# Raising the scheduling priority of the first batch's attention over weights and MoE work in a fused attention and gated-MLP kernel

## The chip, the cores and the metric

The kernel runs on one core of a Trainium2 chip. The metric is device time in microseconds (us) of one execution. Before the change three runs gave 489.43 us as the median, from 487.89 to 490.92 us. Five engines work side by side on the core, each with its own queue of instructions that it takes strictly in the order in which they were written: TensorE (PE, matmuls; PEld is its weight load), VectorE (DVE), ScalarE (ACT), GpSimd (POOL), and SyncE (SP), which here only starts transfers.

## The reference

The inputs are four batches of eight heads, 768 tokens of 64 numbers. Each query sees the 4 first tokens (sinks) and the last 128. The attention output, 768 x 512 per batch, goes through a gated MLP ("MoE" in the code).

```python
scores = scale * np.matmul(q, k.transpose(0, 1, 3, 2))
keep = is_sink | in_window                    # is_sink: pos < 4; in_window: 0 <= rel < 128
scores = np.where(keep, scores, -1000000000.0)
a = np.exp(scores - np.max(scores, axis=-1, keepdims=True))
a = a / (np.sum(a, axis=-1, keepdims=True) + 1e-09)
x = np.matmul(a, v)                           # then (B, S, H * D)
h = np.maximum(x @ w_in, 0.0)                 # 512 -> 1024
conv_out = ...                                # three taps along the tokens, weights conv_w
gate = 1.0 / (1.0 + np.exp(-conv_out))
return (h * gate @ w_out).astype(np.float32)  # 1024 -> 512
```

## The kernel before

**Attention.** The heads go in pairs, four pairs to a batch, and a pair's 768 queries in six tiles of 128, three to a half. A tile passes through three functions. `scores` multiplies on PE (tile `sc`, line 339 in the first batch, 342 and 343 later), masks and takes the minimum on DVE (lines 508 and 509), takes exponentials on ACT (512), sums and inverts on DVE (514, 515) and normalizes on POOL (517), into `pe`. `transp` turns `pe` on PE (532, tile `pts`), copies it out on ACT (534, tile `pT`) and cuts the band out of the copy with two selects on POOL (536, 538). After the third tile of a half `pv` multiplies by the values (573 and 576, tile `px`), and `xout` splits the result into a high and a low part, `xH` on ACT (350) and `xL` on DVE (351), the input of the MLP. A tile's `transp` is written one step after its `scores`, its `pv` two steps after. In batch 0 the first halves of all four pairs come first, then the second halves: 24 steps.

**Weights.** `w_in` and `w_out` come from HBM as 64-bit floats in 16 pieces of 128 x 512 (and the taps). A piece is narrowed (`narrow`: 111 on ACT; 112, 113, 114 on DVE) and split into a high part (121 on ACT) and a low part (122, `wiL` on POOL, `woL` on DVE). The list `WHEN` asks for one piece a step from step 2 on. The temporaries (`stm`) have three buffers.

**MLP.** It is cut into units of 256 tokens and 128 hidden columns: 12 matmuls into `ph` (183), the gate on ACT (190, 194, 197), DVE (195, 196, 198) and POOL (200, 201, tile `g`), and six matmuls into `po` (210) two units later. A unit of the first 256 tokens needs the first halves of all four pairs. The pieces of the units are written between the attention steps at an even rate, from the middle of batch 0 on.

**What sets the order.** The program is written in the order of the loop in `banded`, each step in three slots. A scheduler then walks through it, with a model of its own of how long things take, and fixes each engine's order: of the instructions that are ready in its model, the one with the better priority goes first, and priority is the place in the written program. What stands in a queue is never passed on the chip by what stands behind it.

Of the kernel before, what the change touches and what calls it, by code (L numbers as in the profile page):

```python
# [31 lines left out]
TRAIL = 2  # L32
NGB = TRAIL + 2
LA = 1
WHEN = list(range(2, 19))


# [360 lines left out]
def banded(c):  # L398
# [159 lines left out]
    def pv(g, t):  # L558

        s = st[g]  # L560
        hp = g % NPAIR
        hf, u = divmod(t, 3)
        if u < 2:
            return
        px = ps.tile([P, 3, P], F32, tag="px", name=f"px{g}_{hf}").rearrange("p t k -> p (t k)")
        first = 3 * hf
        tiles = range(first + 2, max(0, first - 1) - 1, -1)
        for kt in tiles:
            pT = s.pT.pop((kt, hf)).rearrange("p h a k -> p h (a k)")
            lo, hi = max(kt, first), min(kt + 1, first + 2)  # L570
            cols = slice(P * (lo - kt), P * (hi - kt) + P)
            for j in range(2):
                nc.tensor.matmul(px[D * j:D * j + D, P * (lo - first):P * (hi - first) + P], s.v[:, kt, j, :], pT[:, j, cols],  # L573
                                 start=(kt == tiles[0]), stop=False, skip_group_check=True)
        for w in range(1 - hf, 3):
            nc.tensor.matmul(px[:, P * w:P * w + P], (vsr if g >= NPAIR else c.vs)[:, w, P * hp:P * hp + P], s.sT, start=False, stop=(w == 2),  # L576
                             skip_group_check=True)
        A.xout(g, hf, px)
# [40 lines left out]
    steps = [(n, g, 3 * half + u) for n, (g, half) in enumerate(jobs) for u in range(3)]  # L619
    NST = len(steps)  # L620
    NSTB = NPAIR * T
    D1, D2 = 1, 2
# [7 lines left out]
    for i in range(NST + D2):  # L630
        if i < NST:
            n, g, t = steps[i]
            if t % 3 == 0:
                for n1, lo, hi in coming(n):
                    new = prep(n1)
                    todo += [(i + lo + (hi - lo) * (k + 1) / len(new), x) for k, x in enumerate(new)]
            if g >= NPAIR or t % 3 == 2:
                fetch()
            if t == 0 and g and g % NPAIR == 0:
                after = i + 3 if g > NPAIR else i  # L640
            if i == after:
                sink_split(c, m, vsr, g // NPAIR)
            if n + 1 < len(jobs) and (t % 3 == 2 if n < 2 * NPAIR else t == 3):
                values(n + 1)
        if i == NSTB // 2:
            clear()
        m.need(min(sum(i >= w for w in WHEN), len(m.todo)))
        for slot in range(SLOTS):
            if slot == 0 and i < NST:
                scores(g, t)  # L650
            if slot == 1 and 0 <= i - D1 < NST:
                transp(*steps[i - D1][1:])
            if slot == 2 and 0 <= i - D2 < NST:
                pv(*steps[i - D2][1:])
                if i - D2 + 1 in cuts:
                    while fill:
                        fill.pop(0)()
                    lo, hi, span = cuts[i - D2 + 1]
                    fill = m.pieces(lo, hi)
                    rate = len(fill) / (span - 0.5)  # L660
                    acc = 0.0
            acc += rate / SLOTS
            while acc >= 1.0 and fill:
                fill.pop(0)()
                acc -= 1.0
            while todo and i + (slot + 1) / SLOTS >= todo[0][0]:
                todo.pop(0)[1]()
# [143 lines left out]
```

## Time and profile before

| | us |
|---|---|
| median of three runs | 489.43 |
| the profiled execution | 490.03 |
| its span in the profile | 488.3 |
| TensorE busy in the span | 457.4 (94%) |
| VectorE busy | 348.4 (71%) |
| ScalarE busy | 340.5 (70%) |
| GpSimd busy | 312.7 (64%) |
| mean granted TensorE clock, share of full speed | 0.983 |

The span leaves 1.73 us of the profiled execution outside it. The profiled execution took 0.60 us more than the median. Busy shares are means over the whole span; the first quarter and the rest differ, so they are read by stretch.

### The profile page before, as it was taken

What the parts mean: (1) busy time and instruction counts of PE and PEld (TensorE: products, weight loads), DVE (VectorE), ACT (ScalarE), POOL (GpSimd) and SP (SyncE); (2) the same over time, 40 slices, a digit from 0 to 9 for tenths busy, and PEclk for the clock granted to TensorE, in tenths of its full rate; (3) what the DMA queues carried; (4) which work ended last, traced back from release to release, by engine and by line L of the source; (5) the groups of instructions that cost most, each with busy time, mean ns of one, the idle gap of its engine ahead of it and who ended that gap; (6) DMA issues with size and microseconds to landing.
All of it is one profiled execution on the core that took longest, in us unless ns stands there. A gap on an engine that the chain in (4) does not pass through costs nothing.

```text
span 488.3 us, 10470 instructions
## 1 busy us (share of the span) xinstructions
PE 457.4 (94%) x3149; PEld 389.7 (80%) x3149; DVE 348.4 (71%) x1212; ACT 340.5 (70%) x1086; POOL 312.7 (64%) x614
## 2 busy tenths in 40 slices
PE   2887798899999999999999999999999999999995
PEld 2555477688889888888888888888888888999993
DVE  4798989957968777786677585886675665656553
ACT  3887858778878977786877786876776754545451
POOL 3584796867976867684758577685764564344441
PEclk9988989999999999999999999999999999999998
DMA  5778653537234132334132332324021100101011
GB/s 147 211 229 212 172 168 79 126 85 188 67 72 116 61 83 66 87 96 99 60 77 58 85 81 60 70 63 98 24 55 33 44 3 0 44 2 44 1 44 53
DMA packets 87307, 41.03 MB, mean 84 GB/s; under 512 B 80160, under 2 KB 80184, under 8 KB 87240
## 3 DMA queue, kind: packets, MB, share of 16 engines
q1 hardware_dynamic: 87096, 39.99, 31.5%
q8 instruction: 28, 0.46, 0.4%
q14 instruction: 39, 0.32, 0.2%
q10 hardware_dynamic: 144, 0.26, 0.2%
HBM read 27.60 MB, written 6.29 MB: 69 GB/s over the span
## 4 chain that ended last, share of the span: by engine, by line
PE 80%; DVE 7%; DMA 3%; issue 3%; ACT 2%; POOL 2%; SPq 1%; DVEq 0%; ACTq 0%; POOLq 0%
PE po L210 27%; PE ph L183 26%; PE px L573 8%; PE sc L342 4%; PE pts L532 4%; PE sc L343 3%; PE px L576 2%; PE tq L276 2%; PE tk L294 2%; PE sc L339 2%; POOL pe L517 1%; DVE sc L508 1%; DMA wi_1r<-in_moe_w_in_dram 1%; DVE pe L509 1%; DVE stm L113 1%
## 5 line engine op out<-in xcount | busy, mean ns | idle before, releaser
L210 PE MATMUL po<-woH,g 128*128 128x512 f32 x384 | 142.0, 409 | 1.2 <-POOL g L200 1.0
L183 PE MATMUL ph<-xH,wiH 128*128 128x258 f32 (+1 forms) x384 | 112.2, 292 | 1.2 <-ACT X L255 1.2
L183 PE MATMUL ph<-xH,wiL 128*128 128x258 f32 (+1 forms) x384 | 109.0, 284 | 0.0
L183 PE MATMUL ph<-xL,wiH 128*128 128x258 f32 (+1 forms) x384 | 108.8, 284 | 0.0
L517 POOL TENSOR_SCALAR pe<-pe,sm 128x132 f32<-128x132 f32 (+1 forms) x192 | 82.8, 442 | 34.9 <-DVE sm L515 27.2
L512 ACT ACTIVATE pe<-pe,sm 128x132 f32<-128x132 f32 (+1 forms) x192 | 77.5, 406 | 15.8 <-DVE sm L509 14.7
L200 POOL TENSOR_SCALAR g<-t 128x256 fp32r<-128x256 f32 x96 | 42.2, 439 | 70.7 <-DVE t L198 50.8
L195 DVE SCALAR_TENSOR_TENSOR t<-hb,cw,t 128x256 f32<-128x256 f32 x96 | 54.0, 562 | 36.6 <-ACT t L194 36.1
L201 POOL TENSOR_TENSOR g<-t,g 128x256 fp32r<-128x256 f32 x96 | 75.2, 784 | 5.6
L210 PEld LDWEIGHTS po<-woH,g 128*128 128x128 f32 x384 | 68.7, 189 | 11.6 <-POOL g L200 2.6
L183 PEld LDWEIGHTS ph<-xH,wiH 128*128 128x128 f32 x384 | 73.0, 190 | 5.5 <-ACT X L255 1.6
L210 PE MATMUL po<-woL,g 128*128 128x512 f32 x192 | 76.4, 398 | 0.0
L183 PEld LDWEIGHTS ph<-xH,wiL 128*128 128x128 f32 x384 | 72.9, 190 | 2.1
L183 PEld LDWEIGHTS ph<-xL,wiH 128*128 128x128 f32 x384 | 72.8, 190 | 0.7
L197 ACT ACTIVATE t<-t 128x256 f32<-128x256 f32 x96 | 40.1, 418 | 33.8 <-DVE t L196 33.4
L198 DVE SCALAR_TENSOR_TENSOR t<-t,hb 128x256 f32<-128x256 f32 x96 | 47.5, 494 | 20.1 <-ACT t L197 19.0
L508 DVE COPY_PREDICATED sc<-before,sc 128x128 f32<-128x128 int32 x160 | 45.6, 291 | 22.6 <-PE sc L343 19.1
L509 DVE CUSTOM_DVE_ANT_0 pe<-sc,m 128x132 f32<-128x132 f32 (+1 forms) x192 | 54.0, 288 | 10.3 <-PE sc L343 7.8
L190 ACT ACTIVATE hb<-ph 128x258 f32<-128x258 f32 (+1 forms) x96 | 37.0, 386 | 31.4 <-PE ph L183 30.7
L536 POOL TENSOR_SCALAR_AFFINE_SELECT pT<-pT 128x256 f32<-128x256 f32 x80 | 38.2, 477 | 31.4 <-ACT pT L534 31.1
L196 DVE SCALAR_TENSOR_TENSOR t<-hb,cw,t 128x256 f32<-128x256 f32 x96 | 54.1, 564 | 4.1
L194 ACT ACTIVATE t<-hb,cw 128x256 f32<-128x256 f32 x96 | 49.2, 513 | 7.7 <-POOL g L201 3.9
(124 smaller groups left out, 930.2 us busy)
## 6 DMA issues: line engine op xcount, KB each, us to landing
raw<-in_q_dram SPq DMA_DIRECT2D x64, 96.0 KB
raw<-in_k_dram SPq DMA_DIRECT2D x64, 96.0 KB
out_dram<-stm SPq DMA_DIRECT2D x23, 256.0 KB
kk<-kk SPq DMA_DIRECT2D x24, 198.0 KB
vraw<-in_v_dram SPq DMA_DIRECT2D x24, 192.0 KB
wi_0r<-in_moe_w_in_dram SPq DMA_DIRECT2D x2, 512.0 KB
wi_1r<-in_moe_w_in_dram SPq DMA_DIRECT2D x2, 512.0 KB
wi_2r<-in_moe_w_in_dram SPq DMA_DIRECT2D x2, 512.0 KB
```

Source lines behind the costliest of these rows:

```text
L183: nc.tensor.matmul(u.h[:, 0:W], w[:, cc, ff * P:(ff + 1) * P], x[:, cc, t0:t1], start=(i == 0), stop=(i == len(prods) - 1))
L194: nc.scalar.mul(a, prev, cw[:, 0, ff:ff + 1])
L195: nc.vector.scalar_tensor_tensor(out=e, in0=this, scalar=cw[:, 1, ff:ff + 1], in1=a, op0=ALU.mult, op1=ALU.add)
L196: nc.vector.scalar_tensor_tensor(out=a, in0=nxt, scalar=cw[:, 2, ff:ff + 1], in1=e, op0=ALU.mult, op1=ALU.add)
L198: nc.vector.scalar_tensor_tensor(out=a, in0=e, scalar=1.0, in1=this, op0=ALU.add, op1=ALU.mult)
L200: nc.gpsimd.tensor_scalar(u.g[:, 0], a, 1.0, 1.0, ALU.mult, ALU.mult)
L201: nc.gpsimd.tensor_tensor(out=u.g[:, 1], in0=a, in1=f(u.g[:, 0]), op=ALU.subtract)
L210: nc.tensor.matmul(po[:, 0:c.DM], u.g[:, a, tt * P:(tt + 1) * P], w[:, ff, :], start=(ff == 0 and i == 0), stop=(ff == NFF - 1 and i == 2))
L508: nc.vector.copy_predicated(pc[:, KW:SW], before.bitcast(I32), pc[:, 0:P])
L509: nc.vector.tensor_tensor_reduce(out=pe[:, j, cols], in0=pc[:, P:SW][:, cols], in1=mk, op0=ALU.add, op1=ALU.min, scale=1.0, scalar=3.0e38, ...
L512: nc.scalar.activation(pe[:, j, cols], pe[:, j, cols], AF.Exp, bias=sm[:, j:j + 1], scale=-1.0, accum_out=sm[:, 2 + 2 * j:3 + 2 * j])
L517: nc.gpsimd.tensor_scalar(pe[:, j, cols], pe[:, j, cols], sm[:, 8 + j:9 + j], 1.0, ALU.mult, ALU.mult)
```

## The change

The body of `scores`, `transp` and `pv` is now issued inside a block that gives its instructions a priority 300 places better than where they are written, for the 24 steps of batch 0 (`NSTB` is 24). From batch 1 on the offset is 0. Nothing is added or removed: the same instructions run, with the same operands, and `transp` and `pv` still belong to tiles one and two steps back. The weights, the loading and turning of later pairs (`prep`) and the MLP's pieces keep their old priority.

```diff
+AHEAD = 300
 ...
         for slot in range(SLOTS):
-            if slot == 0 and i < NST:
-                scores(g, t)
-            if slot == 1 and 0 <= i - D1 < NST:
-                transp(*steps[i - D1][1:])
+            with c.tc.high_priority(offset=AHEAD if i < NSTB else 0):
+                if slot == 0 and i < NST:
+                    scores(g, t)
+                if slot == 1 and 0 <= i - D1 < NST:
+                    transp(*steps[i - D1][1:])
+                if slot == 2 and 0 <= i - D2 < NST:
+                    pv(*steps[i - D2][1:])
             if slot == 2 and 0 <= i - D2 < NST:
-                pv(*steps[i - D2][1:])
```

The lines of the changed kernel have numbers one higher than before (517 is 518 there). Three places follow; each shows one engine's queue, first before, then changed.

GpSimd, at the end of the first half of pair 2 (its scores are `pe_0_421`, its turned tiles 480, 531 and 561) and in the midst of pair 3's (`pe_0_545`, turned tiles 604, 654, 687). Before:

```order
L517 TENSOR_SCALAR pe_0_421<-pe_0_421,sm_166 128x132 x2
L517 TENSOR_SCALAR pe_0_545<-pe_0_545,sm_167 128x128 x2
L536 AFFINE_SELECT pT_0_0_480<-pT_1_0_531 128x2x128
L538 AFFINE_SELECT pT_1_0_531<-pT_1_0_531 128x2x128
L517 TENSOR_SCALAR pe_0_545<-pe_0_545,sm_163 128x132 x2
L536 AFFINE_SELECT pT_1_0_531<-pT_2_0_561 128x2x128
L517 TENSOR_SCALAR pe_0_545<-pe_0_545,sm_164 128x132
L538 AFFINE_SELECT pT_2_0_561<-pT_2_0_561 128x2x128
L517 TENSOR_SCALAR pe_0_545<-pe_0_545,sm_164 128x132
```

Changed:

```order
L518 TENSOR_SCALAR pe_0_421<-pe_0_421,sm_166 128x132 x2
L539 AFFINE_SELECT pT_2_0_437<-pT_2_0_437 128x2x128
L537 AFFINE_SELECT pT_0_0_480<-pT_1_0_531 128x2x128
L539 AFFINE_SELECT pT_1_0_531<-pT_1_0_531 128x2x128
L537 AFFINE_SELECT pT_1_0_531<-pT_2_0_561 128x2x128
L518 TENSOR_SCALAR pe_0_545<-pe_0_545,sm_167 128x128 x2
L539 AFFINE_SELECT pT_2_0_561<-pT_2_0_561 128x2x128
L518 TENSOR_SCALAR pe_0_545<-pe_0_545,sm_163 128x132 x2
L537 AFFINE_SELECT pT_0_0_604<-pT_1_0_654 128x2x128
L539 AFFINE_SELECT pT_1_0_654<-pT_1_0_654 128x2x128
L518 TENSOR_SCALAR pe_0_545<-pe_0_545,sm_164 128x132 x2
```

The select that finishes pair 2's last turned tile (line 538 on 561) now stands ahead of two tiles of pair 3's normalization (`sm_163`, `sm_164`), of which three instructions stood ahead of it.

GpSimd again, where the first two units of the MLP (`g_808`, `g_869`) meet the low parts of `w_in`'s second half (`stm_704` and `stm_762` are its last two pieces). Before:

```order
L122 TENSOR_TENSOR wiL<-stm_660,wiH 128x512
L517 TENSOR_SCALAR pe_1_670<-pe_1_670,sm_167 128x132 x2
L200 TENSOR_SCALAR g_808<-t_801 128x256
L201 TENSOR_TENSOR g_808<-t_801,g_808 128x256
L517 TENSOR_SCALAR pe_1_826<-pe_1_826,sm_163 128x132 x2
L200 TENSOR_SCALAR g_869<-t_862 128x256
L536 AFFINE_SELECT pT_4_1_792<-pT_5_1_847 128x2x128
L201 TENSOR_TENSOR g_869<-t_862,g_869 128x256
L122 TENSOR_TENSOR wiL<-stm_704,wiH 128x512
L538 AFFINE_SELECT pT_5_1_847<-pT_5_1_847 128x2x128
L517 TENSOR_SCALAR pe_1_826<-pe_1_826,sm_164 128x132 x2
L122 TENSOR_TENSOR wiL<-stm_762,wiH 128x512
```

Changed:

```order
L123 TENSOR_TENSOR wiL<-stm_704,wiH 128x512
L537 AFFINE_SELECT pT_4_1_792<-pT_5_1_847 128x2x128
L539 AFFINE_SELECT pT_5_1_847<-pT_5_1_847 128x2x128
L201 TENSOR_SCALAR g_808<-t_801 128x256
L518 TENSOR_SCALAR pe_1_826<-pe_1_826,sm_163 128x132 x2
L202 TENSOR_TENSOR g_808<-t_801,g_808 128x256
L123 TENSOR_TENSOR wiL<-stm_762,wiH 128x512
L201 TENSOR_SCALAR g_869<-t_862 128x256
L202 TENSOR_TENSOR g_869<-t_862,g_869 128x256
L518 TENSOR_SCALAR pe_1_826<-pe_1_826,sm_164 128x132 x2
```

The two low parts of the weights and the attention's selects now stand ahead of the MLP's `g` that they stood behind.

VectorE at the start, the first tile of pair 0 (`pe_0_206`) and the first piece of weights (`stm_257`). Before:

```order
L436 TENSOR_SCALAR m_139<-m_139 128x132
L509 ISA pe_0_206,sm_163<-sc_0_0_208,m_137 128x128
L509 ISA sm_163 128x1
L112 TENSOR_SCALAR stm_257<-stm_258 128x512
L509 ISA pe_0_206,sm_163<-sc_0_1_209,m_137 128x128
L509 ISA sm_163 128x1
L113 SCALAR_TENSOR_TENSOR stm_257<-wi_0r,stm_257 128x512
```

Changed:

```order
L437 TENSOR_SCALAR m_139<-m_139 128x132
L113 TENSOR_SCALAR stm_257<-stm_258 128x512
L510 ISA pe_0_206,sm_163<-sc_0_0_208,m_137 128x128
L510 ISA sm_163 128x1
L114 SCALAR_TENSOR_TENSOR stm_257<-wi_0r,stm_257 128x512
L510 ISA pe_0_206,sm_163<-sc_0_1_209,m_137 128x128
L510 ISA sm_163 128x1
```

Here the weights' steps moved ahead of the attention's: the first tile now stands behind the narrowing of the first piece.

Four more moves are told in words. On ScalarE the second piece's high part (line 121) now stands behind the copies of pair 2's turned queries and keys. On SyncE the load of pair 3's second half of keys now stands behind one load of values and two pieces of weights (the last of `w_in`, the fifth of `w_out`). On TensorE twelve matmuls of line 210 (units 0 and 1 of the MLP) stood ahead of the products with the values of pair 0's second half, and now stand behind them. And at the last product of batch 0's attention (`px_1_1493`) 397 instructions stand ahead of it in TensorE's queue before and after; at its low part (line 351) 332 stand ahead on VectorE before and 329 after. The last 330 rows of TensorE's queue are the same.

## Rows read from the trace of the kernel before

**Rows 1.** The page, parts 1 and 2: busy time, and tenths in 40 slices.

```profile
PE 457.4 (94%) x3149; PEld 389.7 (80%) x3149; DVE 348.4 (71%) x1212; ACT 340.5 (70%) x1086; POOL 312.7 (64%) x614
...
PE   2887798899999999999999999999999999999995
...
PEclk9988989999999999999999999999999999999998
```

**Rows 2.** By stretch: length, busy PE PEld DVE ACT POOL, granted clock, DMA.

```profile
12.20:24.40 12.20, 10.11 (x48) 7.18 (x48) 9.42 (x47) 10.90 (x39) 6.80 (x15) 1.00 0.78 211
24.40:97.60 73.20, 60.37 (x356) 45.31 (x355) 66.56 (x215) 56.19 (x178) 55.83 (x88) 0.91 0.61 164
109.40:480.00 370.60, 369.04 (x2635) 322.66 (x2635) 259.14 (x897) 259.90 (x832) 237.07 (x469) 1.00 0.24 62
```

**Rows 3.** Timeline of TensorE: start, length, line; in brackets the idle before.

```profile
41.87 2.40 PE L573 MATMUL px<-pT,vraw 128*64 128x128 f32 x12 [1.73 <-POOL pT L538]
...
50.16 1.30 PE L573 MATMUL px<-pT,vraw 128*64 128x128 f32 x12 [0.64 <-POOL pT L538]
...
57.90 0.68 PE L339 MATMUL sc<-kk,X 128*128 128x260 f32 x2 [1.67 <-DVE sm L509]
59.71 1.21 PE L339 MATMUL sc<-kk,X 128*128 128x260 f32 x2 [1.13 <-DVE sm L515]
61.63 1.21 PE L339 MATMUL sc<-kk,X 128*128 128x260 f32 x2 [0.71 <-DVE sm L509]
...
83.49 0.49 PE L318 MATMUL trk<-ident,raw 128*128 128x128 f32 x3
```

**Rows 4.** Timeline of GpSimd, around the release of pair 2's product.

```profile
38.48 1.31 POOL L517 TENSOR_SCALAR pe<-pe,sm 128x132 f32<-128x132 f32 x2 [0.86 <-ACT xH L350]
...
40.19 1.27 POOL L517 TENSOR_SCALAR pe<-pe,sm 128x132 f32<-128x132 f32 x1
41.42 0.40 POOL L538 TENSOR_SCALAR_AFFINE_SELECT pT<-pT 128x256 f32<-128x256 f32 x1
```

**Rows 5.** Busy time by stretches of 2 us, columns as in the second group.

```profile
40.00:42.00 2.00, 0.27 (x4) 0.13 (x4) 1.64 (x5) 1.57 (x4) 1.97 (x4) 0.94 1.22 287
42.00:44.00 2.00, 2.00 (x12) 1.07 (x12) 1.65 (x4) 0.79 (x2) 0.34 (x1) 0.50 0.86 258
44.00:46.00 2.00, 2.00 (x11) 1.74 (x10) 0.57 (x2) 0.59 (x2) 0.00 (x0) 0.70 1.09 265
...
62.00:64.00 2.00, 2.00 (x7) 1.51 (x7) 2.00 (x5) 0.64 (x4) 1.92 (x3) 0.50 0.36 57
64.00:66.00 2.00, 2.00 (x10) 1.67 (x9) 2.00 (x10) 1.67 (x6) 2.00 (x4) 0.58 0.55 205
```

**Rows 6.** Waits in 24 to 97 us: us in total, times, longest.

```profile
DVE stm L112 <- POOL wiL L122: 1.8, 1, 1.8
```

**Rows 7.** Timeline of GpSimd, the two low parts of the weights.

```profile
67.28 1.28 POOL L122 TENSOR_TENSOR wiL<-stm,wiH 128x512 fp32r<-128x512 f32 x1
...
70.20 1.53 POOL L122 TENSOR_TENSOR wiL<-stm,wiH 128x512 fp32r<-128x512 f32 x1
```

**Rows 8.** Timelines of VectorE and ScalarE at the start, and one SyncE issue.

```profile
10.31 0.29 DVE L509 CUSTOM_DVE_ANT_0 pe<-sc,m 128x128 f32<-128x128 f32 x1
...
11.60 0.28 DVE L509 CUSTOM_DVE_ANT_0 pe<-sc,m 128x128 f32<-128x128 f32 x1
...
12.45 0.16 DVE L514 TENSOR_REDUCE sm<-sm 128x2 f32<-128x4 f32 x1
...
17.36 0.62 ACT L121 CAST wiH<-stm 128x512 fp32r<-128x512 f32 x1 [1.14 <-DVE stm L114]
...
55.93 0.34 SPq L100 DMA_DIRECT2D wo4r<-in_moe_w_out_dram  x1
```

**Rows 9.** Line 114: busy us and mean ns; its min/median/max ns.

```profile
L114 DVE SCALAR_TENSOR_TENSOR stm<-stm,stm 128x512 int32<-128x512 int32 x16 | 14.2, 887 | 0.0
...
L114 DVE SCALAR_TENSOR_TENSOR stm<-stm,stm x17: 675/690/1751, 12.5 to 83.1; 128x512 int32<-128x512 int32 x16, 24x128 int32<-24x128 int32 x1
```

## The prediction

> **What bounds the kernel now.** The first view is the page's busy times and slices. TensorE is busy for 457.4 of 488.3 us, and its row of slices reads 9 nearly throughout from the ninth slice on, while the first eight hold 7s and 8s [rows 1]. So the end of the kernel is set by TensorE's work plus the time that TensorE loses, and nearly all of that loss lies in the first 100 us. The view by stretch puts sizes to it. From 109.4 to 480 us TensorE is busy for 369.04 of 370.60 us, which leaves 1.56 us to win. From 24.4 to 97.6 us it is busy for 60.37 of 73.20 us, at a granted clock of 0.91; VectorE is busy for 66.56 us there, 91% [rows 2]. This early stretch is thus bound by the engines around TensorE, VectorE first, with waits between them, and later TensorE eats a backlog of MLP work that never runs dry. Since the change leaves as many instructions of TensorE ahead of batch 0's last product as before (397), and 329 for 332 on VectorE, batch 0 costs TensorE the same work: whatever time this stretch becomes shorter or longer by moves the end by the same time. A softmax that is early gains nothing by itself.
>
> The second view is TensorE's own timeline in the stretch, for what ended its waits. Two places stand out: the product of pair 2 at 41.87 us, which had waited 1.73 us for a select on GpSimd, and three pairs of scores from 57.90 to 61.63 us, which had waited 1.67, 1.13 and 0.71 us for VectorE, 3.51 us together [rows 3].
>
> **The change, part by part.** No instruction is added or removed, so every term is a wait that moves.
>
> *Pair 2's product.* Its releaser is the select that started at 41.42 us and lasted 0.40. Ahead of it GpSimd ran three normalizations of pair 3: two in 1.31 us from 38.48, one in 1.27 us from 40.19 [rows 4]. The new order puts these behind the select, so up to 1.31 + 1.27 = 2.58 us. Pair 3 needs them too, but the whole core is nearly empty behind this wait: from 42 to 46 us GpSimd is busy for 0.34 us of 4 [rows 5]. The MLP cannot start before pair 3's product at 50.16 us [rows 3], and that one follows from pair 2's through the queues of TensorE and ScalarE. What this may win is bounded by VectorE, the next that is late: it is idle for 6 - (1.64 + 1.65 + 0.57) = 2.14 us between 40 and 46 [rows 5], and is nearly full elsewhere. I take this, **-2.1 us**; the ends are 0 (another input of the select, its copy on ScalarE, is late) and -2.6.
>
> *The low parts of the weights.* VectorE waited once, for 1.8 us, for such a part on GpSimd [rows 6], because the two passes of 1.28 and 1.53 us at 67.28 and 70.20 us [rows 7] stood behind the MLP's `g`. They now stand ahead of it. But GpSimd has as much to do as before, and `g` and the normalization that follow them become later, with the products of line 210 behind those. I take half, **-0.9 us**, between 0 and -1.8.
>
> *The start.* VectorE's first pass over scores began at 10.31 us. It now stands behind the narrowing of the first weights, whose first step was over when the second pass began at 11.60, so 1.29 us later; the second goes from 11.60 to about 12.45, 0.85 later [rows 8]. Behind it wait the exponentials, and GpSimd and TensorE behind those. Against this stands that ScalarE at 17.36 us had waited 1.14 us for the same kind of step [rows 8], in front of the copies of pair 2's queries and keys, and these now go first. What covers the delay is VectorE's idle time from 12.2 to 24.4 us, 12.2 - 9.42 = 2.78 us [rows 2]. I take **0**, with ends of +0.9 (the cover is gone) and -1.1.
>
> *The transfers.* SyncE's queue now issues pair 3's second keys behind a piece of weights that was issued at 55.93 us [rows 8]; they are turned on TensorE at 83.49 us [rows 3]. That is 27 us to spare, and costs nothing; it would cost a transfer's time if the buffers of the weights came free that much later.
>
> *From batch 1 on.* The offset is 0. The queues differ in places, as the scheduler starts from another state, but TensorE has 1.56 us of idle time in all there [rows 2], and its last 330 rows are the same: 0.
>
> The sum is -2.1 - 0.9 + 0 = **-3.0 us**. Made against the profiled execution, that is 488.3 + 1.73 = 490.03 to 487.0 us; the median of the runs is 0.60 us below that execution, so the forecast is 489.4 - 3.0 = **486.4 us**, 0.6% faster. About 1%, 4.9 us, is what a measurement of this kernel can tell from no change, so this counts as no difference.
>
> **The rivals.** *The gain is taken back* (489.2 us). From 62 to 66 us VectorE is busy all 4 us and GpSimd for 3.92 [rows 5]. If the MLP starts earlier it meets this stretch earlier and still has to wait for the same passes. Worse, VectorE's passes are stretched in places: line 114 takes 690 ns as its median but up to 1751, and 887 on average [rows 9], so 16 x 0.197 = 3.2 us are lost already by this line alone. An order that sets more of these passes beside GpSimd's could lose as much again, and -3.0 + 3.2 = +0.2 us would be left; if the rest is merely not won, some -0.5 us; I put the case at -0.2. The Trainium skill, page "GPSIMD Engine Reference", section "1. Specifications", says that GpSimd shares its SBUF interfaces with VectorE and that VectorE instructions with two SBUF inputs contend there; line 114 reads two such tensors, and its spread agrees. By that rule the earlier low parts of the weights buy little. For this rival: the totals on each engine are unchanged. Against it: the 2.14 us at 40 to 46 us are idle, not slow.
>
> *The clock stays up* (483.0 us). The granted clock is 0.50 and 0.70 from 42 to 46 us and 0.50 and 0.58 from 62 to 66 us, each time after a stretch where TensorE did little (0.27 us of 2 from 40 to 42), and TensorE is busy throughout both [rows 5]. At full clock the same work takes 2 x (0.50 + 0.30) = 1.60 us and 2 x (0.50 + 0.42) = 1.84 us less, together 3.4. If both gaps ahead of them shrink enough, this comes on top of the sum: -6.4 us. For it: the first gap is the one that the first term closes. Against it: at 42 to 46 us this counts the same time as the first term in part, and at 62 us VectorE is full. The Trainium skill, page "TensorE: Matmul & The Clock Gate", section "What's actually happening", says that the throttled clock is the default and that activity releases it; the rows agree in both places.
>
> *TensorE starves in the second half of batch 0* (493.4 us, slower). The new order holds twelve matmuls of the MLP behind pair 0's second product. Where TensorE stood for scores from 57.9 to 61.6 us it lost 3.51 us with no other work ahead in its queue [rows 3]. With attention first and MLP behind it, the same can happen at the product of each pair until the backlog is long enough; at two more pairs it costs 2 x 3.51 = 7.0 us, and -3.0 + 7.0 = +4.0 us. It decides as soon as more than one such wait is added. For it: MLP units are what fills TensorE while VectorE is full, and they come later in the queue. Against it: in that place the new queue sets twelve matmuls of line 183 between one tile's scores and the next.
>
> That the priority does nothing at all can be left out, since the queues differ on every engine; that it does little is the first rival.
>
> **How the numbers follow.** The forecast gets 0.50, the gain taken back 0.25, the clock 0.15, the slower case 0.10. The likeliest gives **486.4 us**. The range leaves out the slower case and the far part of the clock's: its lower end is 482.5 us, 0.5 below the clock's case, which also holds all terms at their good ends (-2.6 - 1.8 - 1.1 = -5.5, 483.9). Its upper end is all terms at their bad ends, +0.9, with the spread of the runs (490.92 is the highest): 491.0 us. Faster by over 1% means below 484.5: the clock's case and a small part of the forecast's, 0.20. Slower by over 1% means above 494.3: most of the slower case, 0.08. Within 1%: 0.72.
>
> **What the changed profile would show.** First term: pair 2's product starts at about 39.3 us instead of 41.87, its select runs ahead of pair 3's normalizations, and pair 3's product starts at about 47.6 instead of 50.16, both 2.58 us earlier. Second: VectorE's wait of line 112 for line 122 is gone. Start: the first scores are read near 11.6 us, and the product of pair 0 is where it was, within 1 us. The stretch from 24.4 to batch 0's last product is some 3 us shorter, with TensorE's busy time and count about the same, and behind it nothing has changed but the time. The forecast is wrong if pair 3's product is early and the last product of batch 0 isn't (the first rival), if the granted clock stays at 1.00 from 40 to 66 us (the second), or if TensorE waits over 3 us more for scores and selects between 60 and 100 us (the third).

## The result, and the profile after

The changed kernel takes 485.05 us (median of seven runs, 483.84 to 486.60); the kernel before took 489.43 us beside it (seven runs). The ratio is 0.9907, with a 95% interval of 0.9885 to 0.9929: about 4.4 us faster, 0.9%. The forecast was 486.4 us in a range of 482.5 to 491.0 us.

The page of the profiled execution (483.84 us, span 482.1), the lines that answer to [rows 1]:

```profile
PE 455.0 (94%) x3149; PEld 386.9 (80%) x3149; DVE 343.9 (71%) x1212; ACT 338.9 (70%) x1086; POOL 316.0 (66%) x614
...
PE   2878898999999999999999999999999999999995
...
PEclk9989999999999999999999999999999999999999
```

The counts are those of before; TensorE is busy 2.4 us less, and the clock's row has two 8s where it had four. To see where the span went, it is cut at the first matmul of batch 0's last product: at 109.37 us before, at 105.45 us with the change. The view by stretch (length, then busy time and count of PE, PEld, DVE, ACT and POOL, granted clock, DMA); the third row of each ends with TensorE's work, 8.2 us before the span's end. Before:

```profile
0.00:109.37 109.37, 85.87 (x507) 65.66 (x507) 88.43 (x315) 80.00 (x254) 74.46 (x143) 0.94 0.60 158
109.37:488.30 378.93, 371.49 (x2643) 324.03 (x2642) 260.01 (x898) 260.52 (x833) 238.21 (x471) 1.00 0.24 63
109.37:480.10 370.73, 369.17 (x2635) 322.79 (x2635) 259.27 (x897) 259.93 (x832) 237.07 (x469) 1.00 0.24 62
```

Changed:

```profile
0.00:105.45 105.45, 84.65 (x507) 63.68 (x508) 87.46 (x314) 80.18 (x252) 77.11 (x144) 0.97 0.62 161
105.45:482.10 376.65, 370.31 (x2642) 323.22 (x2642) 256.44 (x900) 258.69 (x835) 238.85 (x471) 1.00 0.25 64
105.45:473.90 368.45, 368.02 (x2635) 321.99 (x2635) 255.75 (x899) 258.10 (x834) 237.71 (x469) 1.00 0.25 64
```

The same 507 matmuls stand in front of the cut. That part is 3.92 us shorter: 2.70 us of TensorE's idle time (23.50 to 20.80) and 1.22 us of its busy time. But the part behind the cut is shorter too, by 2.28 us, with as many matmuls: 1.13 us of idle time (1.56 to 0.43) and 1.15 us of busy time. The prediction had 3.0 us in front and nothing behind.

TensorE's timeline with the change, the rows that answer to [rows 3]:

```profile
39.96 0.55 PE L319 MATMUL trk<-ident,raw 128*128 128x128 f32 x3 [0.17 <-ACT sT L549]
40.44 1.30 PE L574 MATMUL px<-pT,vraw 128*64 128x128 f32 x12
...
45.29 0.68 PE L533 MATMUL pts<-ident,pe 128*128 128x128 f32 x2 [1.81 <-POOL pe L518]
47.73 2.40 PE L574 MATMUL px<-pT,vraw 128*64 128x128 f32 x12
...
58.40 1.11 PE L340 MATMUL sc<-kk,X 128*128 128x260 f32 x4 [0.53 <-DVE sm L516]
```

Pair 2's product is 1.43 us earlier and no longer waits for its select; it stands behind turned keys. Pair 3's is 2.43 us earlier, behind a wait of 1.81 us for its own normalization. The three pairs of scores that had waited 3.51 us for VectorE have become groups of four that waited 0.53. GpSimd's timeline, beside [rows 4]:

```profile
37.73 1.67 POOL L518 TENSOR_SCALAR pe<-pe,sm 128x128 f32<-128x128 f32 x2
39.36 0.41 POOL L539 TENSOR_SCALAR_AFFINE_SELECT pT<-pT 128x256 f32<-128x256 f32 x1
40.54 1.48 POOL L518 TENSOR_SCALAR pe<-pe,sm 128x132 f32<-128x132 f32 x2 [0.77 <-DVE sm L516]
```

The select runs 2.06 us earlier, behind pair 3's first tile and no longer behind its second and half of its third. The waits of TensorE from pair 3's product to the cut (total us, times, longest). Before:

```profile
PE sc L339 <- DVE sm L509: 3.5, 4, 1.7
PE sc L339 <- DVE sm L515: 1.8, 2, 1.1
```

Changed:

```profile
PE pts L533 <- POOL pe L518: 1.5, 3, 0.6
PE pts L533 <- ACT pT L535: 0.8, 1, 0.8
...
PE sc L340 <- DVE sm L516: 0.5, 1, 0.5
```

So 5.3 us of waiting for VectorE have become 0.5, and 2.3 us of waits for the inputs of transposes stand in their place. Where the front is won shows best at pair 1's second product: it starts at 81.27 us before and at 80.36 us with the change (81.98 in the repeat below), so little or nothing of what the earlier products won is left there. From there to the cut TensorE has nearly as many matmuls, but idles for 2.27 us before and for 0.31 with the change, and VectorE has 83 instructions to do before and 76 with the change. Before, then changed:

```profile
81.27:109.37 28.10, 25.83 (x178) 21.04 (x177) 22.35 (x83) 21.83 (x73) 19.91 (x39) 1.00 0.40 93
80.36:105.45 25.09, 24.78 (x176) 20.88 (x176) 19.16 (x76) 20.56 (x67) 20.51 (x40) 1.00 0.40 91
```

### The profile page after: what moved, and what is told of

Its sections match the earlier page's. It is cut to its first block, busy times and chain, and to the rows that moved or that the text cites. A ratio compares the mean times of both kernels' runs of the same rounds, so it can differ in the third digit from the quotient of the medians.

```text
span 482.1 us, 10496 instructions
## 1 busy us (share of the span) xinstructions
PE 455.0 (94%) x3149; PEld 386.9 (80%) x3149; DVE 343.9 (71%) x1212; ACT 338.9 (70%) x1086; POOL 316.0 (66%) x614
## 4 chain that ended last, share of the span: by engine, by line
PE 79%; DVE 5%; ACT 5%; POOL 4%; DMA 4%; issue 2%; SPq 1%; ACTq 0%; DVEq 0%; POOLq 0%
PE ph L184 27%; PE po L211 26%; PE px L574 8%; PE pts L533 4%; PE sc L343 4%; PE sc L344 3%; PE tq L277 2%; PE px L577 2%; DMA raw<-in_q_dram 2%; ACT pe L513 2%; PE tk L295 1%; POOL pe L518 1%; DVE stm L115 1%; DMA wo0r<-in_moe_w_out_dram 1%; PE sc L340 1%
## 5 line engine op out<-in xcount | busy, mean ns | idle before, releaser
L518 POOL TENSOR_SCALAR pe<-pe,sm 128x132 f32<-128x132 f32 (+1 forms) x192 | 86.4, 462 | 33.8 <-DVE sm L516 22.0
L201 POOL TENSOR_SCALAR g<-t 128x256 fp32r<-128x256 f32 x96 | 43.5, 453 | 72.4 <-DVE t L199 39.9
L202 POOL TENSOR_TENSOR g<-t,g 128x256 fp32r<-128x256 f32 x96 | 73.7, 768 | 5.3
```

The source lines that it names most:

```text
L201: nc.gpsimd.tensor_scalar(u.g[:, 0], a, 1.0, 1.0, ALU.mult, ALU.mult)
L202: nc.gpsimd.tensor_tensor(out=u.g[:, 1], in0=a, in1=f(u.g[:, 0]), op=ALU.subtract)
L518: nc.gpsimd.tensor_scalar(pe[:, j, cols], pe[:, j, cols], sm[:, 8 + j:9 + j], 1.0, ALU.mult, ALU.mult)
```

## The experiments

Each kernel was compared with the kernel before on the same chip (there 490.4 to 490.7 us). "In front" is the time to the first matmul of batch 0's last product, "behind" the time from there to the span's end, both from one profiled execution.

| kernel | median us | ratio (95%) | in front | behind |
|---|---|---|---|---|
| before | 489.43 | | 109.37 | 378.93 |
| changed | 485.05 | 0.9907 (0.9885, 0.9929) | 105.45 | 376.65 |
| e0_again | 485.12 | 0.9901 (0.9878, 0.9925) | 106.61 | 376.79 |
| e1_first_half | 486.60 | 0.9948 (0.9928, 0.9968) | 107.03 | 377.77 |
| e2_second_half | 488.99 | 0.9977 (0.9965, 0.9990) | 109.00 | 376.80 |
| e8_scores | 490.98 | 1.0014 (0.9995, 1.0033) | 108.44 | 381.06 |
| e9_transp_pv | 489.87 | 0.9992 (0.9982, 1.0002) | 109.81 | 378.29 |
| e16_select | 491.79 | 1.0027 (1.0010, 1.0044) | 110.94 | 379.56 |
| e23_block_zero | 487.71 | 0.9943 (0.9922, 0.9964) | 109.58 | 375.72 |
| e22_batch0 | 487.28 | 0.9937 (0.9914, 0.9961) | 106.55 | 378.75 |
| e5_all | 488.81 | 0.9974 (0.9957, 0.9991) | 106.13 | 380.67 |
| e20_first | 485.40 | 0.9892 (0.9867, 0.9917) | 106.64 | 377.16 |
| e10_whole | 528.86 | 1.0796 (1.0760, 1.0832) | 106.63 | 419.77 |
| e17_before_whole | 517.67 | 1.0556 (1.0528, 1.0585) | 109.56 | 405.34 |

**The change again.** No edit.

> The changed kernel once more, on the same chip as the next three. All theories: ratio 0.989 to 0.993, some 485 us. In the profile the last product of batch 0 starts near 105.5 us; if the 2.3 us that the first profile gained behind that product were of that one execution, the part behind it is again near 378 to 379 us instead of 376.7.

Behind the cut the two executions agree within 0.14 us. In front they differ by 1.16 us with one and the same queue; e22_batch0, e20_first and e10_whole have that queue too, and stand at 106.55 to 106.64. The typical gain in front is thus 2.8 us against the one profile of the kernel before, and the 3.92 us of the first profile is the high one. Each kernel below has one profile, so a difference of less than about 1.2 us between two fronts shows nothing by itself.

**One half of batch 0 at a time.**

```diff
-            with c.tc.high_priority(offset=AHEAD if i < NSTB else 0):
+            with c.tc.high_priority(offset=AHEAD if i < NSTB // 2 else 0):               # e1_first_half
+            with c.tc.high_priority(offset=AHEAD if NSTB // 2 <= i < NSTB else 0):       # e2_second_half
```

> The priority holds for the 12 steps of the first halves alone. The queues are those of the change up to the product of pair 3's first half. Theory A (the gain is made where the first halves of pairs 2 and 3 end, and all the rest follows): ratio 0.990 to 0.994, pair 3's product at 47.7 us. Theory B (the gain is made in the second half, by MLP matmuls that now stand between the scores): 0.996 to 1.001. Theory C (any other order gives or takes some us, there is no such place): anywhere from 0.985 to 1.010.

> The priority holds for the 12 steps of the second halves alone. The queues are those of before up to the first MLP units. Theory A: ratio 0.997 to 1.003, pair 3's product at 50.2 us and the clock down from 58 to 66 us as before. Theory B: 0.990 to 0.994. Theory C: anywhere from 0.985 to 1.010, and the two halves' gains do not add up to the whole.

In front, the first twelve steps alone win 2.34 us, the last twelve 0.37, which is less than that difference. Pair 3's product is at 48.12 us with e1_first_half and at 50.14 with e2_second_half; by this run the moves of the second half are worth little. Behind the cut both are faster than before, e2_second_half by 2.13 us although its last twelve steps moved the cut by 0.37 only: the first sign that the gain behind has a cause of its own.

**One function at a time.** The cut is shortened: e8_scores takes transp and pv out of the block, e9_transp_pv takes scores out instead.

```diff
             with c.tc.high_priority(offset=AHEAD if i < NSTB else 0):
                 if slot == 0 and i < NST:
                     scores(g, t)
-                if slot == 1 ...: transp(...)     # e8_scores: these two outside the block;
-                if slot == 2 ...: pv(...)         # e9_transp_pv: these two inside, scores outside
```

> Only the scores and softmax have the priority, not the transposes and products. The queues are those of the change until past pair 3's first product; later they differ. Theory A: 0.990 to 0.994. Theory B: 0.990 to 1.000, since the second half's queues differ. Theory C: anywhere from 0.985 to 1.010.

> The changed kernel, with transp and pv alone inside the block; scores are issued outside it with the old priority. VectorE's queue holds as much work of the weights and the MLP ahead of the low part of pair 0's second half as before: 54 passes over weights and 9 of the gate (with the change 50 and 7, with scores alone 51 and 8).
> Theory V (what is won in front of batch 0's last product is won where VectorE stands between pair 3's product and pair 0's second one, and the scores' priority is what moves passes over weights and gates behind it): the first-half products are those of before within 0.5 us, pair 0's second product is at 69 to 71 us instead of 63, the last product within 1 us of 109.4.
> Theory G (GpSimd: selects and products that go first are the gain): the last product is at 107 us or earlier, as with the change.
> Behind the last product theory P, with the block around two of three functions, expects a queue of its own and says only that the time lies within 375 to 381 us; the run is 487 to 491 us by V and 484 to 488 us by G.

With the scores alone the products of pairs 2 and 3 come at 40.59 and 47.80 us, as with the change, and TensorE no longer waits for scores there; yet the last product gains 0.93 us only, less than two executions of one queue differ (in their place stand a wait of 1.8 us for the MLP's `g` and one of 1.7 us for a copy), and behind it 2.13 us are lost. With transposes and products alone all is as before up to the cut (pair 0's second product at 69.68 us), as theory V said. So neither part alone makes the gain in front: the scores' priority moves VectorE's work, and the gain is only seen where transposes and products have the priority too. Theory A comes near for the two halves (0.9948 where it said at most 0.994, and 0.9977 inside its range) but misses e8_scores (1.0014 where it said at most 0.994); theory B misses both halves.

**The first term alone.** The select is moved without any priority. The scheduler orders the queues anew behind this move, so it is not the only difference: 501 matmuls stand in front of the cut, not 507.

```diff
+            if (g, t) == (2, 2):
+                c.sel = sel                        # the select that ends pair 2's last turned tile
 ...
+        with c.tc.issue_after(c.sel.ins) if g == 3 and t in (1, 2) else nullcontext():
             for j in range(2):
                 nc.gpsimd.tensor_scalar(pe[:, j, cols], ...)
```

> The kernel before, with one move alone: the normalizations of pair 3's second and third tile are held in GpSimd's queue behind the select that finishes pair 2's last turned tile. No priority is changed.
> The first term of the prediction: pair 2's product starts at about 39.3 us instead of 41.87, pair 3's at about 47.6 instead of 50.16, the last product of batch 0 is 2.1 us earlier (107.3 instead of 109.4), and the run is 2.1 us shorter, 488.3 (by theory Q the new neighbours behind batch 0 add another -0.3).
> Rival (the gain of this move needs the rest of the change): the products of pairs 2 and 3 are early, but the last product of batch 0 is at 109 us and the run at 490, because VectorE is full in the second half.
> Second rival (the clock): pair 2's product comes after a shorter gap and runs at full clock, another -1.1 us.

TensorE's timeline of this kernel:

```profile
39.73 1.30 PE L576 MATMUL px<-pT,vraw 128*64 128x128 f32 x12 [0.86 <-POOL pT L539]
...
46.96 1.30 PE L576 MATMUL px<-pT,vraw 128*64 128x128 f32 x12
...
52.49 0.68 PE L339 MATMUL sc<-kk,X 128*128 128x260 f32 x2 [0.67 <-DVE sm L509]
55.52 0.68 PE L339 MATMUL sc<-kk,X 128*128 128x260 f32 x2 [1.33 <-DVE sm L509]
57.33 1.02 PE L339 MATMUL sc<-kk,X 128*128 128x260 f32 x2 [1.14 <-DVE sm L509]
60.34 0.83 PE L533 MATMUL pts<-ident,pe 128*128 128x128 f32 x2 [1.99 <-POOL pe L518]
```

Both products are earlier than with the change, at full clock, and 3.20 us are won at pair 3's. But TensorE then stands 3.14 us for the same scores as before (3.51 us there), and 1.99 us for a normalization. Behind these waits 2.69 us are still won (pair 0's second product at 67.00 us for 69.69); they are lost by pair 1's second product (81.91 for 81.27), and the last one is at 110.94, 1.57 us later than before. VectorE's wait for a low part of the weights on GpSimd [rows 6] is 2.9 us here, 1.8 before. The run is 0.27% longer. So the gain is taken back, as in the first rival of the prediction, but not by stretched passes: line 114's 16 passes take 12.7 us here and 14.2 before.

**The block without the offset.** The next two tell what happens behind the cut.

```diff
-AHEAD = 300
+AHEAD = 0                                                            # e23_block_zero
 ...
-            with c.tc.high_priority(offset=AHEAD if i < NSTB else 0):
+            with c.tc.high_priority(offset=AHEAD) if i < NSTB else nullcontext():   # e22_batch0
```

> The changed kernel with an offset of 0 in batch 0 too: the block stands around scores, transp and pv in all steps, and raises nothing by its number. TensorE's queue is that of the kernel before for 142 rows, up to the second product of pair 0, and differs behind that, though no offset does; the queue behind batch 0 holds 30 pieces of products and 37 transposes next to a product (before 32 and 41, changed 32 and 31).
> Theory P (the block itself, at offset 0, moves the queue from batch 1 on, and that is where the changed kernel's gain behind batch 0's last product, 2.1 to 2.3 us, comes from; the gain in front of it comes from the 300): the first-half products are those of before (25.7, 36.0, 41.9, 50.2 us), the last product of batch 0 stands within 1 us of 109.4, and behind it the kernel takes 376.8 instead of 378.9 us: 488.3 us.
> Theory S (what is won behind batch 0 is won by the order and the backlog that batch 0 leaves behind): the time behind it is that of before, and the run is 490.5 us.

> The changed kernel without the block from batch 1 on: the steps of batch 0 have the offset of 300, and later steps are issued as in the kernel before. TensorE's queue is the changed kernel's to well past the last product of batch 0. Behind it are 35 pieces of products and 32 transposes next to a product.
> Theory P: the last product of batch 0 is at 105.5 to 106.6 us as with the change, and behind it the time is that of the kernel before, 378.9 us instead of 376.7: 487.3 us.
> Theory S: 485.1 us, as with the change.

Theory P held on both sides (behind the cut 375.72 us for 376.8 expected, and 378.75 for 378.9). The rows of e23_block_zero:

```profile
0.00:109.58 109.58, 85.97 (x507) 65.94 (x507) 87.77 (x315) 80.30 (x254) 75.41 (x143) 0.95 0.59 158
109.58:485.30 375.72, 369.53 (x2643) 323.68 (x2642) 257.68 (x898) 258.81 (x833) 239.01 (x471) 1.00 0.25 63
109.58:477.10 367.52, 367.22 (x2635) 322.44 (x2635) 256.98 (x897) 258.23 (x832) 237.86 (x469) 1.00 0.25 63
```

And of e22_batch0:

```profile
0.00:106.55 106.55, 84.75 (x507) 64.40 (x507) 88.15 (x314) 80.23 (x252) 75.29 (x144) 0.97 0.60 159
106.55:485.30 378.75, 371.85 (x2642) 322.82 (x2642) 260.31 (x900) 258.55 (x835) 237.20 (x471) 1.00 0.25 63
```

With a block and no offset the front is that of before and 3.21 us are won behind. With the offset in batch 0 and no block later, the front is that of the change and nothing is won behind (378.75 for 378.93). Each gain comes without the other, and by the runs they add up within their intervals: 0.57% and 0.63% alone, 0.93% and 0.99% together. A block of offset 0 is thus no empty edit: an empty one leaves the queue as it was, but one around the attention changes TensorE's queue from its 143rd row on. The scheduler sets its count of places back when a block ends, so what is written behind the block (the MLP's pieces, the turning of later pairs) takes places as good as the block's own. It did not keep its old priority, as the section on the change has it.

**Priority in all batches.**

```diff
-            with c.tc.high_priority(offset=AHEAD if i < NSTB else 0):
+            with c.tc.high_priority(offset=AHEAD):
```

> The changed kernel with the better priority in all four batches, not in the first alone. TensorE's queue is the changed kernel's for its first 261 rows of some 300 up to the last product of batch 0; behind that 30 pieces of products instead of 32, and 35 transposes next to a product instead of 31.
> Theory Q: the neighbours come out nearly even (+0.1 us), so the run is that of the changed kernel, 485 us within 1.
> Theory W (waits): attention that goes first in every batch makes the MLP's work late; TensorE has a backlog, so nothing is won (485), and what is lost shows as idle time at the end of a batch, up to 489.

The front is 106.13 us, but behind it 4 us are lost against the change, though the neighbours in TensorE's queue come out even; TensorE's idle time there is 2.73 us for 0.43, and the rest of the 4 us is busy time. Theory Q failed here, and theory W's warning held.

**Whole products.** Two ways to keep each product of batches 1 to 3 in one piece: a block that waits as one (on the changed kernel and on the one before), and a priority.

```diff
+        with c.tc.tile_critical() if g >= NPAIR else nullcontext():         # e10_whole, e17_before_whole
+        with c.tc.high_priority(offset=3000 if g >= NPAIR else 0):          # e20_first
             for kt in tiles:
                 ...
                     nc.tensor.matmul(px[...], s.v[:, kt, j, :], pT[:, j, cols], ...)
```

> The changed kernel, with the matmuls of each product with the values of batches 1 to 3 issued as one block that nothing of TensorE's queue stands inside. Nothing is added or left out; the queue is the changed kernel's up to the last product of batch 0. In it, behind that product, a product is cut into 25 pieces instead of 32 (the sink part 25 instead of 31), and a transpose stands next to a product 12 times instead of 31.
> Theory Q (the time behind batch 0 is set by what stands next to what in TensorE's queue): in the traces so far a piece of a product costs some 0.1 us on top of its matmuls where it begins and where it ends, most next to transposes; a sum over the kinds of neighbours in six traces gives -4.0 us for this queue. TensorE's busy time there falls from 368.0 to about 364, and the run to about 481 us.
> Theory W (the time behind batch 0 is waits for other engines, and TensorE's pace there is a matter of what the matmuls are): busy time stays 368 within 0.5; a block that can't be passed makes TensorE wait for its last input, so 485 to 489 us, with idle time behind batch 0 up from 0.4 us.

> The kernel before, with the same edit: the products of batches 1 to 3 as blocks. Behind batch 0's last product 25 pieces instead of 32, and 14 transposes next to a product instead of 41.
> Theory Q: -4.7 us by the same sum, TensorE's busy time behind the last product falls from 369.2 to about 364.5, the run from 490.4 to about 486; and what is left between this kernel and the changed kernel with whole products is the part in front of the last product, 3 to 4 us, with at most 1 us from behind it.
> Theory W: 490 to 493 us, and busy time as before, 369 within 0.5.

> The changed kernel, with the matmuls of the products of batches 1 to 3 raised by 3000 places, without a block that waits as one. TensorE's queue is the changed kernel's up to past the last product of batch 0. Behind it the products come in 25 pieces instead of 32, but a transpose stands next to a product 39 times instead of 31.
> Theory Q (what stands next to what in TensorE's queue): the products' own time falls from 35.8 to about 33.9 us, as it did with blocks; eight more transposes beside a product cost about 0.1 us each; together -1.0 us, 484.1 us.
> Theory W (waits for other engines): a product that goes as soon as it can makes no engine earlier that TensorE waits for; what TensorE saves on the products it loses in waits, and the run is 485 to 487 us.

The blocks cost 43 and 26 us behind the cut, and the runs decide nothing between the two theories: TensorE waits in front of the blocks (in e10_whole for 24 us in all), and not only for their inputs. The longest waits of e10_whole, behind the cut:

```profile
PE px L575 <- DVE sk L554: 3.6, 1, 3.6
PE px L575 <- DMA raw<-in_k_dram: 3.0, 1, 3.0
PE px L575 <- DMA out_dram<-stm: 2.7, 1, 2.7
```

The second is a load of keys and the third a store of the MLP's output. e20_first has whole products without that. The row of the products from 112 to 476 us (busy us, mean ns of one), which counts 336 of their matmuls in each kernel: e20_first (25 pieces in the queue), e23_block_zero (30), the change (32) and e22_batch0 (35), in this order.

```profile
L575 PE MATMUL px<-pT,vraw 128*64 128x256 f32 (+1 forms) x336 | 33.9, 341 | 0.3 <-POOL pT L539 0.3
```

```profile
L574 PE MATMUL px<-pT,vraw 128*64 128x256 f32 (+1 forms) x336 | 36.2, 342 | 0.0
```

```profile
L574 PE MATMUL px<-pT,vraw 128*64 128x256 f32 (+1 forms) x336 | 36.5, 342 | 0.0
```

```profile
L574 PE MATMUL px<-pT,vraw 128*64 128x256 f32 (+1 forms) x336 | 37.7, 343 | 0.0
```

By this row a piece more is (37.7 - 33.9) / 10 = 0.38 us for the same matmuls. This is no net price. The rows of one stretch overlap: a matmul is shown for 0.34 us on average while the products' matmuls follow each other by some 0.1 us, so each piece adds the tail of its last matmul, which other work runs beside. Counted behind the cut from each matmul's start to the next start, the products of e20_first hold 2.1 us less than those of the change, and its transposes of `pe` 3.5 us more. The run of e20_first is that of the change. Its last stretch:

```profile
106.64:475.60 368.96, 366.25 (x2635) 321.92 (x2636) 258.68 (x899) 258.90 (x834) 238.67 (x469) 1.00 0.25 63
```

TensorE's busy time fell by 1.77 us (theory Q: 1.0), and its idle time rose from 0.43 to 2.71. Theory W is the one that told the run. None of the twelve kernels beats the change beyond its interval.

## Why the prediction was right, and where it was not

**What bounds the kernel** was read rightly for the front. From pair 3's product to pair 0's second one the view by stretch of the changed kernel says:

```profile
47.73:63.16 15.43, 12.63 (x78) 9.61 (x77) 15.15 (x47) 12.03 (x37) 13.05 (x16) 0.92 0.71 204
```

VectorE is idle for 0.28 us of 15.43. Before, this step took 19.53 us, with VectorE busy for 17.31. In VectorE's queue, 17 passes over weights and 9 of the MLP's gate stand between the low parts of these two products before, 10 and 7 with the change; the others stand ahead of pair 3's product or behind pair 0's. From there to the cut the time grew from 39.68 to 42.29 us. The sum over both is 1.49 us in this execution (0.30 in the repeat).

What the experiments leave as the cause of the front is VectorE's idle time, which the prediction had as the bound of its first term. Idle time of VectorE in us, one profile each:

| kernel | 40 to 46 us | 62 to 81 us | up to the cut |
|---|---|---|---|
| before | 2.15 | 2.35 | 20.94 |
| changed | 0.03 | 0.46 | 17.99 |
| e0_again | 0.04 | 0.45 | 18.02 |
| e1_first_half | 0.03 | 0.30 | 18.95 |
| e8_scores | 0.03 | 0.30 | 21.92 |
| e9_transp_pv | 1.97 | 2.40 | 21.72 |
| e16_select | 1.46 | 3.89 | 24.85 |

The rows of the kernel before, the change and e16_select, in this order:

```profile
40.00:46.00 6.00, 4.27 (x23) 2.94 (x22) 3.85 (x9) 2.94 (x8) 2.31 (x4) 0.72 1.06 270
62.00:81.00 19.00, 17.33 (x105) 14.13 (x104) 16.65 (x43) 12.62 (x36) 16.81 (x22) 0.90 0.56 150
40.00:46.00 6.00, 4.16 (x28) 2.81 (x29) 5.97 (x21) 5.18 (x13) 3.63 (x6) 1.00 0.89 230
62.00:81.00 19.00, 15.92 (x101) 11.65 (x101) 18.54 (x48) 14.05 (x41) 15.39 (x21) 1.00 0.49 120
40.00:46.00 6.00, 5.48 (x41) 4.07 (x38) 4.54 (x14) 4.10 (x11) 4.20 (x7) 1.00 1.00 272
62.00:81.00 19.00, 15.89 (x92) 12.13 (x92) 15.11 (x35) 11.68 (x32) 13.45 (x20) 0.94 0.51 138
```

Wherever the scores of the first halves have the priority, VectorE has work in both places; e8_scores loses it again behind them. With the change it idles 2.95 us less in front of the cut (2.92 in the repeat), where 3.92 us are won (2.76 in the repeat).

**Pair 2's product** (-2.1 us) came in the predicted place: the select is ahead, the wait is gone, pair 3's product is 2.43 us earlier for 2.58 expected, and pair 2's 1.43, since the products of pairs 0 and 1 are some 0.7 us late already and pair 3's keys are turned ahead of it. The size was right too: VectorE's idle time from 40 to 46 us fell by 2.12 us. As a cause this step failed. It took this product's wait for what leaves VectorE idle, and said that whatever this stretch wins, the end wins. With the select alone VectorE still idles there for 1.46 us, and the 3.20 us won at pair 3's product are gone by pair 1's second one (e16_select); with the scores' priority alone it idles for 0.03 (e8_scores). The prediction also called the whole core nearly empty from 42 to 46 us, where TensorE is busy throughout [rows 5]. The scores that wait for VectorE at 57.9 to 61.6 us, which it named without a term, are not where the gain of e16_select is lost, since 2.69 us of it stand behind them.

**The low parts of the weights** (-0.9 us): VectorE's wait of [rows 6] is gone; ScalarE's wait for the same parts (line 112 for line 123) is 3.1 us in four waits, and was 3.2 us. VectorE's idle time from 62 to 81 us fell by 1.9 us, not by half of 1.8. But the moves of the low parts, which lie in the second half, are not what did it. With e1_first_half, which raises the first half alone, that wait is gone too; with e2_second_half VectorE waits 1.9 us at the same line, for ScalarE.

**The start** (0) stayed inside its ends, but not at 0: VectorE's first pass over scores is at 11.47 us for 11.6 expected, pair 0's product at 26.40 us instead of 25.69 (26.57 in the repeat), and pair 1's at 36.71 instead of 35.97. So 0.7 to 0.9 us were lost here, up to the upper end of 0.9.

**From batch 1 on** (0) is the step that failed. It took an offset of 0 for no change, and 1.56 us of idle time for the most that could be won. The block moves the queue at any offset (e23_block_zero: -3.21 us; e22_batch0: -0.18), and TensorE's busy time is itself a matter of the order. The products' row of the kernel before, in the same stretch as the four above, with 32 pieces:

```profile
L573 PE MATMUL px<-pT,vraw 128*64 128x256 f32 (+1 forms) x336 | 37.1, 342 | 0.0
```

From this kernel to e23_block_zero TensorE's busy time behind the cut falls from 371.49 to 369.53 us, by 1.96, and its idle time before the last 8.2 us falls by 1.26 more (1.56 to 0.30). The products' rows (37.1 and 36.2) do not say where, as they overlap with others. Counted from start to start, waits included, the attention's matmuls behind the cut hold 3.2 us less with the change than before and the MLP's 0.9 us more (3.1 less and 0.9 more in the repeat). The Trainium skill, page "Perfetto Trace Analysis", section "Tensor Engine Instruction (MATMUL, LD_WEIGHTS)", says that the end of a matmul in a trace is computed and not observed; so a short wait may show as busy time, and no run here shows how much of the busy time that fell is such waits. Why the attention's matmuls take less in these orders stays open.

**The sum** was right in size for the front, -3.0 for -2.8 in the repeat and -3.92 in the first profile, with terms whose place was right and whose cause was another. The run beat the forecast by 1.4 us. The gain behind the cut, 2.1 to 2.3 us, is more than that; the profile of the kernel before is one of an execution 0.60 us above its median, which is about what is left over. The upper end of the range does not come out of what it is said to be: 490.92 + 0.9 is 491.8, not 491.0. Nothing hung on it.

**The rivals.** Taken back: not with the whole change, but with its first term alone (e16_select) and mostly with the scores alone (e8_scores), as described there. Its mechanism did not decide: the 16 passes of line 114 (now 115) take 15.3 us with the change for 14.2 before, and 12.7 in e16_select. TensorE starving in the second half did not come: in all it waits for 2.3 us there for transposes' inputs, and no product waits more than 0.7 us. The clock came in part, and moved. The prediction counted 42 to 46 and 62 to 66 us; in that trace the granted clock is also below full from 30 to 36 and from 58 to 62 us, so there were three such stretches, and with the change there are two: 32 to 38 and 46 to 50 us, or 54 to 58 and 78 to 82 in the repeat. The stretches of 2 us in the changed kernel:

```profile
44.00:46.00 2.00, 0.68 (x3) 0.49 (x4) 2.00 (x9) 1.19 (x3) 1.47 (x3) 1.00 0.82 206
46.00:48.00 2.00, 2.00 (x11) 1.45 (x12) 1.67 (x8) 1.97 (x8) 1.15 (x2) 0.67 0.75 224
48.00:50.00 2.00, 2.00 (x12) 0.92 (x10) 1.89 (x8) 2.00 (x8) 1.32 (x2) 0.50 0.82 270
```

The repeat, with the same queue:

```profile
44.00:46.00 2.00, 0.71 (x3) 0.51 (x4) 2.00 (x9) 1.09 (x4) 1.34 (x3) 1.00 1.14 269
46.00:48.00 2.00, 1.57 (x14) 1.17 (x14) 1.67 (x8) 1.88 (x8) 1.15 (x2) 1.00 0.75 162
...
54.00:56.00 2.00, 1.37 (x4) 0.91 (x5) 1.93 (x9) 2.00 (x8) 1.57 (x3) 0.62 0.92 271
56.00:58.00 2.00, 2.00 (x9) 1.71 (x8) 2.00 (x5) 1.34 (x5) 1.93 (x3) 0.52 0.65 145
```

The same gap, 0.7 us of work in 2, is followed by the lower level, 1.2 GHz, in one execution; in the other the clock stays at 2.4 GHz there and falls after 54 us instead. The Trainium skill, page "TensorE: Matmul & The Clock Gate", section "What's actually happening", makes the throttled clock the default that activity releases; the first execution agrees, and the two together show that the queue alone does not say where it falls. In front, TensorE's busy time for the same 507 matmuls is 85.87 us before, 84.65 and 84.92 with the change, at a mean granted clock of 0.94 and 0.97. That this 1 us is clock is not shown: with e1_first_half the clock is 0.97 too, and TensorE is busy for 86.17 us.

## What to carry to other kernels

Follow a gain to the next engine that is full: a product that is early by 3 us was worth nothing at the end where VectorE idled no less (e16_select). A priority block at offset 0 is an edit of its own, so compare queues with the block and without the number. Where a saturated engine took the same instructions in another order, the time moved by up to 3 us either way here, so don't book it as 0.

## What the runs showed of the hardware

The row of the products' 336 matmuls reads 33.9 to 37.7 us by how often other work stands between them; this is no net price, since with the fewest pieces (e20_first) the transposes hold more than the products save, and the run is the same. TensorE's granted clock falls in different places in two executions of one queue (32 to 38 and 46 to 50 us, and 54 to 58 and 78 to 82 us), and their fronts differ by 1.16 us.
